# Order of batch 0's second value products in a fused sliding-attention and SiLU kernel

## The chip, the cores and the metric

The kernel runs on one core of one Trainium2 chip. The metric is the device time of one execution in microseconds, taken as the median of the timed runs. Engine names are those of the profile: PE is the matmul engine and PEld its weight load, DVE, ACT and POOL are the vector, scalar and GpSimd engines, SP issues the output stores.

## What is computed

There are 8 batches of 8 heads, 576 positions and 64 dimensions. Four heads use a plain window of 32 keys, four a strided window (every fourth key, 32 of them). The attention output, with its heads side by side, is the input of a two-layer block with SiLU between.

```python
scores = scale * np.matmul(q, k.transpose(0, 1, 3, 2))
mask_plain = (rel >= 0) & (rel < window)                                     # window = 32
mask_dil = (rel >= 0) & (rel < window * dilation) & (rel % dilation == 0)    # dilation = 4
masks = np.stack([mask_plain if h < H // 2 else mask_dil for h in range(H)], axis=0)
scores = np.where(masks[None, :, :, :], scores, -1000000000.0)
attn = np.exp(scores - np.max(scores, axis=-1, keepdims=True))
attn = attn / (np.sum(attn, axis=-1, keepdims=True) + 1e-09)
attn_out = np.matmul(attn, v)
x = np.ascontiguousarray(attn_out.transpose(0, 2, 1, 3)).reshape(B * S, H * D)
h = x @ w_in                       # 4608 x 512 by 512 x 2048
g = h * (1.0 / (1.0 + np.exp(-h)))
out = g @ w_out                    # 2048 x 512
```

## The kernel before, in words

The kernel goes through the batches in order. For each batch the main loop runs the first layer (16 blocks of 128 hidden channels, with SiLU on ACT) and the second layer; the attention of the batches to come is woven into it. What is woven in, and where, is written by hand: `plan_of(b)` files calls under step numbers with `at(step, function, arguments)`, and the layer code calls `plan(step)` ahead of each block. Nothing reorders afterwards: each engine executes its instructions in the order in which the Python code issued them, and waits on semaphores that the framework adds where one instruction needs another's result or its buffer.

Batch 0 comes first, so its attention is cut in two parts along the sequence: part 0 is the positions 0 to 255, part 1 the positions 256 to 575. `z = 0` are the plain heads, `z = 1` the strided ones. The steps of a part are scores, maximum, exponentials (ACT, L574 and L563), normalising (DVE, L596), turning the probabilities (DVE, L612, tile `pt`), the value products and the casts.

- `values0(z, part)` (def at L691) issues the products of `pt` with the values `vw` by `products` (matmul at L643): 64 small matmuls for (z 1, part 1), 44 for (z 0, part 1). The order inside is by key block and then by head. Heads 0 and 1 write the first of two PSUM tiles `x`, heads 2 and 3 the second.
- `finish0(z, part, copies)` (def at L706) copies the two `x` tiles to the f16 tile `xT[z]`, which layer 1 reads. L713 is the copy for z = 1, L718 that for z = 0. For (1, 1) the first tile is copied by ACT and the second by DVE; for (0, 1) both by DVE.
- `layer1_part(f, part, plan)` (def at L739) is layer 1 of batch 0 for one part: matmuls at L754, SiLU at L762. For part 0 one call covers four blocks of 128 channels and has 16 matmuls of 256 columns; it calls `plan` ahead of each block with the step `f + i - 16`. With f = 8 and i = 0 that is step -8, and i = 2 is step -6. For part 1 one call covers two blocks, 8 matmuls of 320 columns.

The calls of layer 1 stand in this order: part 0 with f = 0, 4 and 8; then part 1 with f = 0, 2, 4 and on to 14, with part 0's last call (f = 12) ahead of part 1's f = 12. Part 1's first matmuls thus need all four casts of part 1, and those of part 0 need none of them.

[...] Tiles of the pool `ps` (4 buffers of one bank) hold the `x` tiles, the transposes and the scores of later batches, and the `h` tiles of the very first layer 1 call; tiles of the pool `big` (2 buffers of two banks) hold all other `h` and `o` tiles. In the built program the tiles around the change lie as follows: `x` of (1, 1) in banks 7 and 4, `x` of (0, 1) in banks 6 and 4, the first call's `h` in banks 6 and 5. Bank 4 is used by the second tile of (1, 1) and by the second tile of (0, 1). So the third product of (0, 1), which is the first to write that tile, carries a wait for the DVE copy of the second tile of (1, 1), and its first product a wait for the SiLU that read the first `h`.

`loads_held` (L824) writes one element of `pt` of (1, 1) on POOL, which holds back the loads issued behind it until the products of (1, 1) have read that tile. The loads are the rest of batch 1's q and k, the last quarter of `w_in`, all of `w_out` and batch 1's v.

Of the kernel before, what the change touches and what calls it, by code (L numbers as in the profile page):

```python
# [29 lines left out]
def kernel(  # L30
# [778 lines left out]
    def transposes(at, b, z, step, copies=both):  # L809
        for which in (1, 0):  # L810
            if b >= DT[z]:
                at(step, turn_qk, b, z, which)
                continue
            at(step, transpose, b, z, which, copies)

    def later(at, b, z, steps, copies=(nc.vector.tensor_copy, nc.vector.tensor_copy)):

        for hi in (0, 1):
            at(steps[hi], normal, b, z, hi)
            at(steps[hi], turned, b, z, hi)  # L820
        at(steps[3], values, b, z)
        at(steps[3], finish, b, z, copies)
# [12 lines left out]
    def plan_of(b):  # L835
        ev = {}

        def at(s, fn, *args):
            ev.setdefault(s, []).append((fn, args))

        def all_exps(b, z):
            for hi in (0, 1):
                at(16, exps, b, z, hi)

        if b == 0:

            at(-8, values0, 1, 1)
            at(-8, loads_held)
            at(-8, finish0, 1, 1, (act, dve))
            at(-6, values0, 0, 1)  # L850
            at(-6, finish0, 0, 1)
            at(0, build_mask)
            at(1, load_qk, 2)
            transposes(at, 1, 1, 6)
            at(10, scores, 1, 1, 0)
            at(11, scores, 1, 1, 1)
            at(13, transpose, 1, 0, 1, both)
            at(15, transpose, 1, 0, 0, both)
            at(11, shift, 1, 1, 0)
            at(17, scores, 1, 0, 0)  # L860
            at(19, scores, 1, 0, 1)
            at(15, load_qk, 3)
            at(15, load_v, 2)
            all_exps(1, 1)
            for hi in (0, 1):
                at(20, exps, 1, 0, hi)
            later(at, 1, 1, (20, 21, 24, 27), (act, act))
            later(at, 1, 0, (23, 24, 28, 31), (act, dve))
        elif b == 1:
            at(16, load_v, 3)  # L870
            transposes(at, 2, 0, 4)
            transposes(at, 2, 1, 6)
            at(9, scores, 2, 0)
            transposes(at, 3, 0, 11, (dve, dve))
            at(17, load_qk, 4)
            at(15, scores, 2, 1)
            all_exps(2, 0)
            all_exps(2, 1)
            at(17, scores, 3, 0)
            later(at, 2, 0, (21, 24, 27, 28))  # L880
            at(22, shift, 3, 0, 0)
            at(22, exps, 3, 0, 0)
            at(22, exps, 3, 0, 1)
            later(at, 2, 1, (29, 30, 33, 34), both)
        else:
            if b + 2 < B:
                at(16, load_v, b + 2)
            if b + 1 < B:
                later(at, b + 1, 0, (0, 0, 4, 6))
                transposes(at, b + 1, 1, 7)  # L890
                if b + 3 < B:
                    at(16, load_qk, b + 3)
            if b + 2 < B:
                transposes(at, b + 2, 0, 14)
                at(19, scores, b + 2, 0)
                at(20, exps, b + 2, 0, 0)
                at(20, exps, b + 2, 0, 1)
            if b + 1 < B:
                at(12, scores, b + 1, 1)
                if b + 2 == B:  # L900
                    at(14, shift, b + 1, 1, 0)
                all_exps(b + 1, 1)
                later(at, b + 1, 1, (22, 23, 27, 28))

        def plan(s):
            for fn, args in ev.pop(s, ()):
                fn(*args)

        return plan
# [48 lines left out]
    for b in range(B):  # L958
        plan = plan_of(b)
        if b == 0:  # L960
            for f in range(0, 12, 4):
                layer1_part(f, 0, plan)
            for f in range(0, NFF, 2):
                if f == 12:
                    layer1_part(12, 0, plan)
                layer1_part(f, 1, plan)
        else:
            for f in range(NFF):
                plan(f)
                layer1(b, f)  # L970
        if b == 0:
            layer2_first(plan)
        else:
            layer2(b, plan)
        for s in range(NFF, 3 * NFF):
            plan(s)
# [30 lines left out]
```

## Time and profile before

| what | us |
|---|---|
| median of 3 runs | 304.52 (304.48 to 304.62) |
| the profiled execution | 305.81 |
| its span, first to last instruction | 303.8 |
| PE busy | 292.5 (96%) |
| ACT busy | 203.1 (67%) |
| DVE busy | 192.9 (63%) |
| POOL busy | 118.8 (39%) |

The span is the part of the profiled execution that the trace covers; 2.0 us of the 305.81 lie around it. The granted TensorE clock is 0.999 on average. The chain that ended last is 91% PE and 5% DMA. All the DMA waits in it come before 22.1 us: the loads of q and k and the first two quarters of `w_in`. From 22.1 us on it runs on PE.

In the timeline, a row is a run of equal instructions: its start, the time from the first one's start to the last one's end, engine, line, operation, tiles, shape and count. Brackets give the engine's idle time just before, and what ended it; "issue" stands for nothing that the profile shows.

### The profile page before, as it was taken

What the parts mean: (1) busy time and instruction counts of PE and PEld (TensorE: products, weight loads), DVE (VectorE), ACT (ScalarE), POOL (GpSimd) and SP (SyncE); (2) the same over time, 40 slices, a digit from 0 to 9 for tenths busy, and PEclk for the clock granted to TensorE, in tenths of its full rate; (3) what the DMA queues carried; (4) which work ended last, traced back from release to release, by engine and by line L of the source; (5) the groups of instructions that cost most, each with busy time, mean ns of one, the idle gap of its engine ahead of it and who ended that gap; (6) DMA issues with size and microseconds to landing.
All of it is one profiled execution on the core that took longest, in us unless ns stands there. A gap on an engine that the chain in (4) does not pass through costs nothing.

```text
span 303.8 us, 10280 instructions
## 1 busy us (share of the span) xinstructions
PE 292.5 (96%) x4395; PEld 185.9 (61%) x4395; DVE 192.9 (63%) x357; ACT 203.1 (67%) x683; POOL 118.8 (39%) x182
## 2 busy tenths in 40 slices
PE   2989999999999999999999999999999999999995
PEld 1656754677545774477644775478644775477543
DVE  1895469557997868866893768955893765800012
ACT  3677599775898659965894659976796558246200
POOL 8617326768997295336806086250000000000000
PEclk9999999999999999999999999999999999999999
DMA  8998999999999899399959199390002100210021
GB/s 100 142 196 135 193 205 124 220 154 145 132 163 198 93 71 130 113 111 40 124 72 184 38 60 131 112 121 2 2 37 106 37 2 12 95 37 0 9 97 69
DMA packets 113213, 30.47 MB, mean 100 GB/s; under 512 B 95520, under 2 KB 108688, under 8 KB 113168
## 3 DMA queue, kind: packets, MB, share of 16 engines
q0 software_dynamic: 107840, 20.38, 85.9%
q1 hardware_dynamic: 5328, 9.44, 8.7%
q8 instruction: 34, 0.56, 0.8%
q14 instruction: 11, 0.09, 0.1%
HBM read 40.75 MB, written 9.44 MB: 165 GB/s over the span
## 4 chain that ended last, share of the span: by engine, by line
PE 91%; DMA 5%; POOL 1%; issue 1%; DVE 0%; POOLq 0%
PE o L798 37%; PE h L727 37%; PE h L754 5%; PE o L774 5%; PE x L643 4%; DMA w_in<-in_moe_w_in_dram 3%; DMA gT<-in_q_dram 3%; PE s L364 2%; PE t L283 1%; POOL gT L135 1%; PE s L374 0%; PE ss L364 0%; PE s L390 0%; POOL w_in L191 0%; POOL vw L183 0%
## 5 line engine op out<-in xcount | busy, mean ns | idle before, releaser
L735 ACT ACTIVATE gT<-h 128x576 f16<-128x576 f32 x112 | 72.9, 651 | 63.6 <-PE h L727 63.4
L798 PE MATMUL o<-w_out,gT 128*128 128x512 f16 (+2 forms) x528 | 113.8, 373 | 0.0
L727 PE MATMUL h<-xT,w_in 128*128 128x288 f16 x896 | 113.2, 286 | 0.0
L727 PEld LDWEIGHTS <-w_in 128*128 128x128 f16 x896 | 86.6, 98 | 23.3
L798 PEld LDWEIGHTS <-gT 128*128 128x128 f16 x528 | 50.1, 98 | 56.0
L574 ACT ACTIVATE pe<-ms,nm 128x64 f32<-128x64 f32 x238 | 78.9, 333 | 0.1
L783 DVE COPY ob<-o 128x512 f32<-128x512 f32 (+2 forms) x35 | 23.0, 666 | 51.6 <-PE o L798 50.6
L574 ACT ACTIVATION_READ_ACCUMULATOR pe<-ms,nm 128x1 f32 x238 | 44.5, 187 | 0.0
L152 POOL DMA_DIRECT2D n<-in_k_dram x44 | 31.9, 732 | 26.5 <-DVE kC L337 25.1
L408 DVE SCALAR_TENSOR_TENSOR ms<-s,mask 128x512 f32<-128x512 f32 x28 | 19.2, 686 | 27.5 <-PE s L364 20.9
L152 POOL DMA_DIRECT2D n<-in_q_dram x44 | 31.9, 732 | 4.2 <-DMA n<-in_q_dram 3.5
L174 POOL DMA_DIRECT2D vw<-in_v_dram x32 | 18.3, 578 | 31.3 <-PE x L643 26.5
L596 DVE TENSOR_TENSOR pn<-pe,r 128x640 f16<-128x640 f32 (+2 forms) x32 | 25.3, 792 | 1.1
L183 POOL DMA_DIRECT2D vw<-in_v_dram x32 | 21.2, 667 | 11.5 <-DMA w_out<-in_moe_w_out_dram 8.4
L612 DVE STREAM_TRANSPOSE pt<-pn 128x640 f16<-128x640 f16 (+4 forms) x32 | 24.7, 772 | 1.1
L488 DVE TENSOR_REDUCE nm<-ms 128x10 f32<-128x640 f32 (+1 forms) x28 | 21.9, 786 | 0.9
L754 PE MATMUL h<-xT,w_in 128*128 128x256 f16 (+1 forms) x128 | 18.0, 291 | 1.2 <-DMA w_in<-in_moe_w_in_dram 0.9
L643 PEld LDWEIGHTS <-vw 32*64 32x64 f16 (+1 forms) x1264 | 12.8, 107 | 5.6 <-issue 5.2
L754 PEld LDWEIGHTS <-w_in 128*128 128x128 f16 x128 | 11.9, 99 | 6.0 <-DMA w_in<-in_moe_w_in_dram 2.1
L676 DVE CAST xT<-x 128x288 f16<-128x288 f32 x26 | 10.1, 450 | 8.2 <-PE x L643 8.2
L774 PE MATMUL o<-w_out,gT 128*128 128x512 f16 x64 | 14.7, 380 | 0.0
L643 PE MATMUL x<-pt,vw 32*64 32x64 f16 (+2 forms) x1264 | 14.6, 193 | 0.0
(94 smaller groups left out, 204.2 us busy)
## 6 DMA issues: line engine op xcount, KB each, us to landing
out_dram<-ob SPq DMA_DIRECT2D x35, 256.0 KB, 3.4
n<-in_k_dram POOLq DMA_DIRECT2D x24, 108.0 KB, 4.7
n<-in_q_dram POOLq DMA_DIRECT2D x24, 108.0 KB, 4.5
vw<-in_v_dram POOLq DMA_DIRECT2D x31, 80.0 KB, 3.9
vw<-in_v_dram POOLq DMA_DIRECT2D x32, 72.0 KB, 4.0
w_in<-in_moe_w_in_dram POOLq DMA_DIRECT2D x4, 512.0 KB, 8.3
w_out<-in_moe_w_out_dram POOLq DMA_DIRECT2D x4, 512.0 KB, 14.4
n<-in_k_dram POOLq DMA_DIRECT2D x20, 72.0 KB, 4.5
```

The lines of the kernel that those rows point to most:

```text
L152: nc.gpsimd.dma_start(out=qk[b, z, which][o : o + QB], in_=bass.AP((q, k)[which].tensor, (b * H + z * HH + half * HH // 2) * S * D + x * Q ...
L488: nc.vector.tensor_reduce(out=nm[:, 0:w], in_=ms[:, 0:w], axis=AX.X, op=ALU.max, negate=True)
L574: nc.scalar.activation(pe[:, t, :], src[t], AF.Exp, bias=a["nm", z, hi][:, t : t + 1], scale=k, accum_out=l[:, t : t + 1],)
L596: nc.vector.tensor_tensor(pn[:, 0:w], a["pe", z, hi][:, 0:w], r[:, 0:w, None].broadcast_to([P, w, KB]), ALU.mult)
L612: nc.vector.transpose(out, src)
L643: nc.tensor.matmul(x[h // 2][h % 2 * D : h % 2 * D + D, col : col + wd], vws[b % 2][r, NB + kb * DIL + c if z else kb], turned_cols(b, pt[ ...
L727: nc.tensor.matmul(h[:, half, 0:HS], w_in16[:, c, f * P : f * P + P], xT[c // 2][:, c % 2, half * HS : half * HS + HS], start=(c == cs[0]) ...
L735: nc.scalar.activation(gT[:, f, s0 : s0 + S].rearrange("p (a c) -> p a c", a=2), h[:, :, 0:HS], AF.Silu)
L754: nc.tensor.matmul(hs[i // m][:, i % m, 0 : c1 - c0], w_in16[:, c, (f + i) * P : (f + i + 1) * P], xT[c // 2][:, c % 2, c0:c1], start=(c = ...
L774: nc.tensor.matmul(o, gT[:, f, t * P : (t + 1) * P], w_out16[:, f, :], start=(f == 0), stop=(f == NFF - 1),)
L783: copy(ob, o)
L798: nc.tensor.matmul(o[:, 0, 0:m], gT[:, f, t * P : (t + 1) * P], w_out16[:, f, cols], start=(f == 0), stop=(f == NFF - 1),)
```

## The change

The products of (z 0, part 1) and their two casts are filed under step -8 instead of -6. They are thus issued directly behind the products of (1, 1), `loads_held` and the casts of (1, 1), ahead of all 16 matmuls of `layer1_part(8, 0)` instead of between the 8th and the 9th.

```diff
             at(-8, values0, 1, 1)
             at(-8, loads_held)
             at(-8, finish0, 1, 1, (act, dve))
-            at(-6, values0, 0, 1)
-            at(-6, finish0, 0, 1)
+            at(-8, values0, 0, 1)
+            at(-8, finish0, 0, 1)
             at(0, build_mask)
```

In the built program, DVE, ACT, POOL and SP have the same instructions in the same order as before. On PE the 44 pairs of weight load and matmul of (0, 1) stand ahead of the first 8 pairs of `layer1_part(8, 0)` instead of behind them. One separate wait instruction of PE (ahead of the first matmul of `layer1_part(8, 0)`) is gone. The PSUM banks are those of before.

## Prediction

> **What bounds the kernel now.** I read the page first: PE is busy 96% of the span, and the chain that ended last is PE for 91%.
>
> ```profile
> PE 292.5 (96%) x4395; PEld 185.9 (61%) x4395; DVE 192.9 (63%) x357; ACT 203.1 (67%) x683; POOL 118.8 (39%) x182
> PE 91%; DMA 5%; POOL 1%; issue 1%; DVE 0%; POOLq 0%
> ```
>
> So a change counts only if it moves PE's stream in time. Next I read the chain of waits in order of time over the stretch that is edited (start, us, what):
>
> ```profile
> 23.98 0.64 PE x L643 x61
> 24.62 1.05 PE h L754 x8
> 25.67 0.46 PE x L643 x44
> 26.12 0.87 PE h L754 x7
> 26.99 0.31 issue
> 27.30 1.37 PE h L754 x9
> ...
> 34.01 0.40 PE s L390 x39
> 34.41 0.17 issue
> 34.59 0.23 PE s L390 x9
> ```
>
> The strided products (61 of the 64 are in this row), 8 layer 1 matmuls, the 44 plain products, 7 more matmuls, a hole of 0.31 us, and then the 16th matmul, which is the first of the nine in the 27.30 row. The reader is to see that PE works without a break from 23.98 to 26.99 and that only 0.31 us are lost, and 0.17 us once more at 34.41. Last I read the timeline, for what the other engines do there:
>
> ```profile
> 23.66 2.00 ACT L762 ACTIVATE gT<-h 128x512 f16<-128x512 f32 x3
> 23.70 0.51 DVE L612 STREAM_TRANSPOSE pt<-pn 128x320 uint32<-128x320 uint32 x1
> 24.73 0.49 DVE L713 CAST xT<-x 128x320 f16<-128x320 f32 x1 [0.52 <-PE x L643]
> 25.54 0.44 ACT L713 CAST xT<-x 128x320 f16<-128x320 f32 x1
> 25.60 0.53 PE L643 MATMUL x<-pt,vw 32*64 32x32 f16 x44
> 26.05 0.94 PE L754 MATMUL h<-xT,w_in 128*128 128x256 f16 x7
> 26.18 0.89 DVE L718 CAST xT<-x 128x320 f16<-128x320 f32 x2 [0.97 <-PE x L643]
> 27.30 0.28 PE L754 MATMUL h<-xT,w_in 128*128 128x256 f16 x1 [0.31 <-issue]
> 27.62 1.02 ACT L762 ACTIVATE gT<-h 128x1024 f16<-128x1024 f32 x1 [1.64 <-PE h L754]
> 28.69 0.30 PE L754 MATMUL h<-xT,w_in 128*128 128x320 f16 x1
> ```
>
> The probabilities that the moved products read are turned by 24.21 (23.70 + 0.51), before the strided products end. The cast L713 on DVE runs from 24.73 to 25.22. It empties bank 4, into which the third moved product writes. Before, the 8 matmuls of layer 1 stood between the two, and the product (25.60) came 0.38 us after the bank was free. The two casts L718 end at 27.07.
>
> **The change part by part.** *Nothing is added or removed* except one wait instruction of PE, which I cost at nothing: it stood at 24.6, with the matmul behind it starting as soon as the products had drained. The 44 products keep their 0.45 us (25.60 to 26.05, start to the next matmul's start). The 8 matmuls keep their pace: 24.62 to 25.60 is 0.98 us for eight, of which some 0.11 us is the change to small tiles, so 0.11 us each. No DMA is moved. POOL's write of one element, behind which its loads queue, still waits for the strided products, whose place is unchanged; the 7.71 us that POOL waits before 24.18 stay, and so do its queue and SP's.
>
> *The wait that is now exposed.* Products one and two of the 44 go to bank 6, free since the first SiLU of 23.66 (24.26). The third waits for the DVE cast, so PE stands from about 24.5 to 25.22 and a release. Behind the waiting product stand the other 41 products and all 16 matmuls, none of which PE can put in its place; DVE's next instruction is the cast of these very products, and ACT's next SiLU needs the 16th matmul. DVE and ACT have nothing else to do there (the 0.97 and 1.64 us of idle time in their rows). The release itself is not shown for this pair. Its bounds: the shortest near row is the SiLU of 27.62 + 1.02 = 28.64, whose bank is written by a matmul at 28.69, 0.05 us later; the longest is a PE weight load at 9.48 behind an ACT copy that ended at 9.24, 0.24 us later. I take 0.05, since that row is also a matmul that waits for a PSUM bank while its weights are loaded. So the products go on at 25.27.
>
> *The sum.* 25.27 + 0.45 for the products and the change of tile size = 25.72, first matmul of layer 1. The 16th starts 15 x 0.11 = 1.65 us later, at 27.37. Before it started at 27.30. Shift: +0.07 us, and +0.26 with the long release. The same by differences: the products come 0.33 us earlier (25.60 to 25.27); eight more matmuls stand behind them, 0.87 us without their change of tile size; and the 16th no longer waits from 26.82 (26.05 + 7 x 0.11) to 27.30, 0.48 us. That is -0.33 + 0.87 - 0.48 = +0.06.
>
> *What the hole was.* The 16th matmul carries no wait, so the hole is not the casts: they end at 27.07, and the first instruction that needs them comes after it. PE's instruction stream explains it. The page counts 34 packets on the instruction queue of PE for 4395 + 4395 instructions, one for about 256:
>
> ```profile
> q8 instruction: 34, 0.56, 0.8%
> 27.29:34.58 7.29, 7.09 (x128) 4.85 (x128) 2.96 (x6) 5.45 (x8) 4.39 (x7) 1.00 1.07 159
> ```
>
> The second row is the stretch between the two holes: 128 matmuls and 128 loads, 256 instructions exactly. The two holes thus stand where PE goes from one block of 256 to the next. The packets themselves, by the trace's record of that queue, landed at 25.86 and 33.19, 1.44 and 1.40 us ahead of the two starts. The first was under way from 24.86, behind a border that PE passed at 23.27, in the part that is not edited; the 16th matmul's place in the stream changes by one instruction. So PE may not start it before 27.30 after the change either, and 27.37 is later than that: the hold costs nothing there, and no time can be won there.
>
> [...]
>
> *What comes behind.* The SiLU of these 16 matmuls and the matmul of 28.69 that waits for its bank move by the same 0.07 us; the four casts are done by 26.8 (25.7 + 0.1, two casts in 0.89), before anything needs them, so they are no bound. Of the 0.17 us at 34.41 I can't tell whether it is fixed in time (then it swallows the shift, and the span stays at 303.8) or follows PE's passing of the block before (then the shift goes through). I take the latter, as the packet's transfer (32.30) begins only behind that passing: 303.8 + 0.07 = 303.87. The profiled execution has 2.01 us around its span (305.81 against 303.8) and is 1.29 us above the median of the runs, which the change does not touch; against the median it is 304.52 + 0.07, or 304.6.
>
> **The rivals.** 0.2% is 0.61 us, about what a measurement of this kernel can tell from no change; so the line runs at 303.91 and 305.13.
>
> *Hidden anyway.* The hold at 34.59 is fixed in time: 34.41 + 0.07 is below 34.59, nothing is moved, 304.5. For it: 0.17 us is more than 0.07, and with the long release (0.26) only 0.09 is left. [...]
>
> *The wait isn't there (faster).* If the third product did not have to wait for the cast, products would run on from 24.45, end with the tile change at 24.45 + 0.45 = 24.90, and the 16th matmul would start at 26.55, 0.75 us earlier, if the block of instructions were there: 303.8. For it: the diff takes four changes of tile size down to two and the casts away from the first part 1 matmul. Against: bank 4 is written by both, and the built program has the wait; and the hold at 27.30 would keep the 16th matmul.
>
> *The instructions come later (slower).* PE's blocks are fetched one ahead among POOL's loads. POOL issues four loads of `w_out` from 27.69 on, just behind the hole at 27.30; they land some 2.55 us apart (POOL's waits for them end at 39.59, 42.13 and 44.72). If the shift puts a block's request behind one more of these, PE waits at 34.59 for 2.55 us more: 304.5 + 2.55 = 307.1, and part of one, half say, 305.8. It decides when the request slips by about 0.4 us (27.30 to 27.69). For it: three borders already cost time or nearly so. Against: 0.07 us, 0.26 at most.
>
> **How the numbers follow.** Forecast (wait for the cast, nearly paid back, carried through) 0.55, 304.6, own range 304.5 to 304.8. Hidden anyway 0.23, 304.5. Faster 0.09, 303.8. Slower 0.13, 305.8. The first two are both within 0.2%: 0.78. The range reaches to the faster case's line, 303.9, and a little past the slower line, 305.2, which leaves about 0.2 outside and holds both ends of the release.
>
> **What would show it.** In the timeline after: 2 or so products, then an idle gap of some 0.7 us ended by DVE's cast L713 at 25.22; the other products from about 25.27; 15 or 16 matmuls of L754 in one run from about 25.72; the 16th at 27.37; no hole of 0.31 us; DVE's two casts L718 between 25.8 and 26.8. If the strided products run into the plain ones without a gap, the wait is not there. If the hole at 27.30 is still there and at a later time, the fetch is the bound. If the stream is on time up to 34.4 and late afterwards, look at the hold of 34.59 and at the next one at 68.3.

## The result, and the profile after

The changed kernel takes 305.21 us (median of 13 runs, 304.72 to 306.85), the kernel before 304.48 us (13 runs, 303.81 to 304.87). The ratio is 1.0034, with a 95% interval of 1.0021 to 1.0047: slower, by 0.7 us. The forecast was 304.6 us with a range of 303.9 to 305.2, and no change as the likeliest outcome. The time lies only 0.01 us above that range, but the range reached so far up for the sake of the slower rival; the forecast itself is 0.6 us off.

The single profiled execution of the changed kernel took 305.16 us, with a span of 303.3 us. That span is 0.5 us *shorter* than the 303.8 us of the profile before. A comparison of these two pages alone thus has the wrong sign.

The chain of waits of the changed kernel, in order of time, over the edited stretch (start, us, what):

```profile
22.01 1.92 PE h L754 x16
23.93 0.72 PE x L643 x62
24.65 0.02 issue
24.67 0.50 DVE xT L713
25.17 0.04 issue
25.21 0.52 PE x L643 x41
25.73 2.94 PE h L754 x24
28.67 0.03 issue
28.70 2.33 PE h L754 x16
```

The chain leaves PE once: from 24.65 to 25.21 it runs over DVE's cast L713. This piece is new. Behind it, the products and 24 matmuls of layer 1 run without a hole. The timeline of the same stretch shows who waits:

```profile
24.67 0.49 DVE L713 CAST xT<-x 128x320 f16<-128x320 f32 x1 [0.73 <-PE x L643]
25.21 0.52 PE L643 MATMUL x<-pt,vw 32*64 32x32 f16 x42 [0.63 <-DVE xT L713]
25.67 4.55 PE L754 MATMUL h<-xT,w_in 128*128 128x256 f16 x34
25.78 0.89 DVE L718 CAST xT<-x 128x320 f16<-128x320 f32 x2 [0.62 <-PE x L643]
```

PE sits idle for 0.63 us ahead of the 42 products that are left of the 44. The release by the cast took 0.04 to 0.05 us (25.16 or 25.17 to 25.21), and the two casts L718 end at 26.67.

So the local figures that the prediction gave for this stretch came true, and the result still lay outside its range. The experiments were made to find out why.

### The profile page after: what moved, and what is told of

It reads as the page before. It is cut to its first block, busy times and chain, and to the rows that moved or that the text cites. A ratio compares the mean times of both kernels' runs of the same rounds, so it can differ in the third digit from the quotient of the medians.

```text
span 303.3 us, 10279 instructions
## 1 busy us (share of the span) xinstructions
PE 291.8 (96%) x4395; PEld 186.1 (61%) x4395; DVE 192.6 (63%) x357; ACT 202.9 (67%) x683; POOL 118.7 (39%) x182
## 4 chain that ended last, share of the span: by engine, by line
PE 91%; DMA 5%; POOL 1%; issue 1%; DVE 0%; POOLq 0%
PE o L798 37%; PE h L727 37%; PE h L754 5%; PE o L774 5%; PE x L643 4%; DMA w_in<-in_moe_w_in_dram 3%; DMA gT<-in_q_dram 2%; PE s L364 2%; PE t L283 1%; POOL gT L135 1%; PE s L374 0%; PE ss L364 0%; POOL w_in L191 0%; PE s L390 0%; POOL vw L183 0%
## 5 line engine op out<-in xcount | busy, mean ns | idle before, releaser
L727 PE MATMUL h<-xT,w_in 128*128 128x288 f16 x896 | 113.2, 286 | 0.0
L727 PEld LDWEIGHTS <-w_in 128*128 128x128 f16 x896 | 86.6, 98 | 23.3
L754 PE MATMUL h<-xT,w_in 128*128 128x256 f16 (+1 forms) x128 | 17.6, 291 | 1.3 <-DMA w_in<-in_moe_w_in_dram 1.3
L754 PEld LDWEIGHTS <-w_in 128*128 128x128 f16 x128 | 12.1, 99 | 5.6 <-DMA w_in<-in_moe_w_in_dram 2.3
```

What stands on the lines that cost most here:

```text
L727: nc.tensor.matmul(h[:, half, 0:HS], w_in16[:, c, f * P : f * P + P], xT[c // 2][:, c % 2, half * HS : half * HS + HS], start=(c == cs[0]) ...
L754: nc.tensor.matmul(hs[i // m][:, i % m, 0 : c1 - c0], w_in16[:, c, (f + i) * P : (f + i + 1) * P], xT[c // 2][:, c % 2, c0:c1], start=(c = ...
```

## The experiments

All traces can be put on one scale by counting from the 17th matmul of layer 1, the first one that needs the second quarter of `w_in`. It starts at 22.06 in the first trace of before and at 22.01 in that of the changed kernel. Two later points are used below: the 48th matmul (the last of `layer1_part(8, 0)`, the "16th" of the prediction) and the 57th (the first that waits for that call's SiLU).

### The two kernels again

Copies of both kernels, unchanged, were run for more traces and times.

before_again: 

> The kernel before once more, unchanged, for another profile. Theory A (the hold is not always there): the 0.31 us hole at 27.30 was a matter of that one execution; here the 16th matmul of L754 starts at 26.8 to 27.1 when counted with the first product at 23.91, the part 1 matmuls start by about 27.1, and the change then costs -0.33 + 0.87 = +0.54 us. Theory B (the hold stays, time is lost behind): the hole of about 0.3 us ends near 27.3 again, and the loss of the change lies behind 34 us. Ratio to before 1.000.

after_again: 

> The changed kernel once more, unchanged. Both theories: 0.63 us of idle PE ahead of the third plain product, ended by DVE's cast; 16th matmul 3.40 us behind the first strided product (27.31 against 23.91). Theory A: nothing else differs from before, so the trace behind 28 us has the same steps as in before, later by some 0.5 us. Theory B: a hold behind 34 us that before does not have. Ratio about 1.0025.

Measured: before_again 304.79 us against 304.43 for before, timed beside it (1.0013, 1.0003 to 1.0023); after_again 305.14 (1.0031, 1.0013 to 1.0049). A copy of the same program can thus come out 0.13% apart, which limits what such a ratio can tell.

The chain of waits of before_again, in order of time:

```profile
21.48 1.92 PE h L754 x16
23.40 0.63 PE x L643 x61
24.04 0.98 PE h L754 x8
25.02 0.46 PE x L643 x44
25.47 4.42 PE h L754 x32
```

This is to be held against the rows of before in the prediction. There, the 44 products were followed by 7 matmuls, 0.31 us of "issue", and the rest from 27.30. Here, the same 44 products are followed by 32 matmuls in one piece. The hole is not there. The 48th matmul starts 4.70 us behind the 17th, not 5.24. In after_again it starts 5.31 us behind, as in the first trace of the changed kernel. The 0.63 us of idle PE that were expected there are split: `w_in` came early (17th matmul at 21.07), the first two plain products waited 0.27 us for SiLU on ACT, and the third then 0.18 us for the cast. (The two products fill the time between.) In after_look3 it is 0.30 and 0.15 us.

Each of the two kernels was profiled three more times, to see which of the two executions of before is the rule.

before_look2: 

> The kernel before, one look. Theory A: the 16th matmul of step -8's call comes 4.70 us behind the 17th matmul of layer 1 (the first one behind the second quarter of w_in), without an idle gap, as in before_again, and not 5.24 us as in the profile of before.

before_look3: 

> The kernel before, another look. As before_look2: 4.70 us without the hold, 5.24 with it. With three looks without it the 27.30 of the first profile is the exception.

before_look4: 

> The kernel before, one more look: 4.70 to 4.85 us from the 17th to the 48th matmul without the hold, idle PE near 40 us between 0 and 0.9 us.

after_look2: 

> The changed kernel, one look. Counted from the 17th layer 1 matmul (the first behind the second quarter of w_in) the 33rd comes 3.66 us later, the 48th 5.31 us, against 2.5 to 2.6 and 4.7 to 4.8 in executions of before without the hold. If part of this is paid back at the third border (PE's idle time near 40 us, 0.01 to 0.88 us in before), that idle time is under 0.1 us here, as in after and after_again.

after_look3: 

> The changed kernel, another look: 3.66 and 5.31 us again, idle PE near 40 us under 0.1 us.

after_look4: 

> The changed kernel, a third look: 3.66 and 5.31 us again, idle PE near 40 us under 0.1 us. If it is 0.2 us or more here, the third border does not pay back the loss, and all of it goes through to the end.

Measured, with two later traces (before_third and after_third, below), in us:

| trace | 17th matmul at | 48th, from 17th | 57th, from 17th | idle PE near 40 us | idle PE near 68 us | span |
|---|---|---|---|---|---|---|
| before | 22.06 | 5.24 | 6.63 | 0.01 | 0.34 | 303.8 |
| before_again | 21.48 | 4.70 | 6.08 | 0.12 | 0.07 | 302.2 |
| before_look2 | 21.61 | 4.84 | 6.22 | 0.67 | 0.44 | 303.4 |
| before_look3 | 21.40 | 4.69 | 6.07 | under 0.04 | 0.17 | 301.9 |
| before_look4 | 21.66 | 4.71 | 6.09 | under 0.04 | 0.73 | 302.8 |
| before_third | 21.43 | 4.69 | 6.07 | under 0.04 | 0.09 | 301.8 |
| after | 22.01 | 5.31 | 6.69 | under 0.04 | 0.38 | 303.3 |
| after_again | 21.07 | 5.31 | 6.69 | under 0.04 | 0.50 | 302.5 |
| after_look2 | 21.82 | 5.31 | 6.69 | under 0.04 | 0.40 | 303.1 |
| after_look3 | 20.92 | 5.31 | 6.69 | under 0.04 | 0.67 | 302.7 |
| after_look4 | 22.48 | 5.30 | 6.69 | under 0.04 | 0.48 | 303.9 |
| after_third | 21.60 | 5.31 | 6.69 | under 0.04 | 0.41 | 303.1 |

Two things follow. The hole at 27.30, on which the prediction's sum stood, is in one of six executions of before. And the changed kernel takes 6.69 us from the 17th to the 57th matmul in all six of its traces, where before without the hole takes 6.07 to 6.22: the change costs 0.47 to 0.62 us at this place, every time.

Theory A (the hold is not always there) holds. Theory B asked for the hole at 27.30 in every execution of before and a new hold behind 34 us. The first part is refuted; the second is taken up under what stays open.

### The wait taken away: own_banks

The order of the change is kept. The plain products write the two PSUM tiles of the first layer 1 call (banks 6 and 5) in place of banks 6 and 4. The first added line stands in `layer1_part`, the others in `values0`.

```diff
+            att(0)["h00"] = hs
-            a["x"] = [ps.tile([P, 512], F32, tag="ps", name=f"x_0_{z}_{part}_{hp}") for hp in (0, 1)]
+            a["x"] = [t.rearrange("p a c -> p (a c)") for t in a["h00"]] if part and not z else [
+                ps.tile([P, 512], F32, tag="ps", name=f"x_0_{z}_{part}_{hp}") for hp in (0, 1)
+            ]
```

> The changed order, but the plain products write the two PSUM tiles of the first layer 1 call (banks 6 and 5) instead of banks 6 and 4, so that they wait for SiLU only and not for the DVE cast. If the wait for the cast is what the change costs, the 0.63 us of idle PE go to at most 0.1, and the time falls by 0.5 to 0.6 us against the changed kernel, to 304.6 or less; where the block of instructions is there in time it is below before by 0.2 to 0.4 us (304.1). If the cost lies behind 34 us or in the order itself (casts, ACT), it stays at 305.2.

Measured: 304.52 us (1.0000, 0.9988 to 1.0011), 0.62 below after_again, timed beside it. It is not below before, which the expectation had as a possibility. Its trace doesn't show the gain. `w_in` came early in it (17th matmul at 20.81), and PE waited for SiLU instead:

```profile
23.61 0.20 PE L643 MATMUL h<-pt,vw 32*64 32x32 f16 x2 [0.24 <-ACT gT L765]
24.10 0.52 PE L643 MATMUL h<-pt,vw 32*64 32x32 f16 x42 [0.29 <-ACT gT L765]
```

That is 0.53 us of idle PE where at most 0.1 was expected, and the 48th matmul comes 5.38 us behind the 17th, no sooner than in the changed kernel. So it was run again, side by side with the two kernels.

own_third: 

> Changed order with banks of their own, again. If the cast's wait is the cost: as before_third within 0.1%, 0.4 to 0.7 us below after_third. Trace: if w_in comes as in most executions (17th matmul at 21.4 or later), idle PE ahead of the plain products is under 0.15 us, and the 48th comes 4.7 to 4.9 us behind the 17th instead of 5.31; if w_in comes early (20.8), PE waits for SiLU, as in own_banks.

own_look: 

> The same kernel, one look: as own_third. 4.7 to 4.9 us from the 17th to the 48th matmul where the 17th starts at 21.4 or later, up to 5.4 where it starts at 20.8.

before_third: 

> The kernel before as a kernel of its own, in one call with the two others. 1.000 to 1.0015 against before; the trace has the 48th layer 1 matmul 4.70 to 4.85 us behind the 17th, or 5.24 with the hold.

after_third: 

> The changed kernel again. If the loss is real and not a matter of placing: 1.002 to 1.0035 against before, and 0.3 to 0.7 us above before_third. If it is placing, as with before_again: within 0.1% of before_third. Trace: 5.31 us from the 17th to the 48th matmul.

Measured, against 304.30 for before, timed beside them: before_third 304.42 us (1.0009, 0.9991 to 1.0027), own_third 304.52 (1.0010, 0.9999 to 1.0021), after_third 305.24 (1.0041, 1.0027 to 1.0054). after_third lies 0.82 us above before_third, a little more than the 0.3 to 0.7 expected; own_third lies 0.72 below after_third. The timeline of own_third:

```profile
23.76 0.70 PE L643 MATMUL x<-pt,vw 32*64 32x32 f16 x64
24.30 0.76 PE L643 MATMUL h<-pt,vw 32*64 32x32 f16 x44
24.57 0.49 DVE L715 CAST xT<-x 128x320 f16<-128x320 f32 x1 [0.63 <-PE x L643]
24.98 2.46 PE L757 MATMUL h<-xT,w_in 128*128 128x256 f16 x20
```

(The edit shifts the lines: the cast L713 is L715 here, and the matmul of layer 1 L757.) The plain products now start at 24.30, ahead of the cast's end at 25.06, and need no more than 0.05 us of idle PE on the way. The 17th matmul started at 21.91, so this is an execution with late `w_in`: the 48th comes 4.72 us behind it and the 57th 6.11, as in before. In own_look ACT ended its exponentials 0.38 us later (22.47 against 22.09); PE waited 0.29 us for SiLU, and the 48th came at 5.06, above the 4.9 expected.

One edit that leaves the order as the change made it, and only takes the plain products out of the bank that the cast holds, brings the time back in the timed runs, twice. So the loss hangs on the wait for the cast and not on the order alone. The three traces show how far this goes in one execution: against the changed kernel's 5.31 us to the 48th matmul, the whole delay is gone in own_third (4.72), 0.25 us of it in own_look (5.06), and none in own_banks (5.38), since in the last two the wait for SiLU takes the place of that for the cast.

### The wait made longer: act_bank

The second tile of the plain products was put into the bank that ACT empties behind three SiLUs, not into the one that DVE empties. The lines around the one shown are those of own_banks.

```diff
...
+            a["x"] = [a["h00"][0].rearrange("p a c -> p (a c)"), a["x"][0]] if part and not z else [
...
```

> The changed order, but the second tile of the plain products lies in the bank (7) that ACT empties behind three SiLUs, not in the one that DVE empties (4): the wait is made longer, as ACT's cast ended 0.55 us behind DVE's in the changed kernel (25.72 against 25.16). If the wait for the cast is what the change costs, idle PE ahead of the third product grows from 0.63 to about 1.2 us and the time by some 0.5 us, to 305.6 to 305.8. If other places set the time, it stays at 305.2.

Measured: 306.22 us (1.0056, 1.0038 to 1.0074; 6 runs). Its timeline on PE:

```profile
24.05 0.20 PE L643 MATMUL h<-pt,vw 32*64 32x32 f16 x2 [0.44 <-ACT gT L765]
25.77 0.20 PE L643 MATMUL x<-pt,vw 32*64 32x32 f16 x2 [1.52 <-ACT xT L715]
26.29 5.01 PE L757 MATMUL h<-xT,w_in 128*128 128x256 f16 x26
```

Idle PE is 1.52 us, more than the 1.2 expected. ACT's cast ended at 25.72, as in the changed kernel, but `w_in` came early in this trace (17th matmul at 21.05), so the products stood ready sooner. The time is 0.4 to 0.6 above what was expected too. The windows tell why (us, then each engine's busy time and count, then the granted clock, DMA share and GB/s):

```profile
24.00:26.00 2.00, 0.43 (x31) 0.38 (x35) 0.32 (x1) 1.72 (x3) 2.00 (x4) 1.00 0.69 96
26.00:28.00 2.00, 2.00 (x46) 1.46 (x34) 1.48 (x5) 0.00 (x0) 2.00 (x3) 0.52 0.93 138
28.00:30.00 2.00, 2.00 (x13) 1.44 (x12) 0.81 (x3) 0.21 (x1) 2.00 (x4) 0.63 1.18 173
```

The third number from the right is the granted clock. In the trace it falls to half from 26.07 to 29.48, 3.41 us, behind the long idle time. The six runs fall into two groups: three with a mean clock of 0.994, the traced one among them, took 306.55 to 306.75 us, three with 1.0 took 305.64 to 305.89. The second group is the wait alone, within the 305.6 to 305.8 expected but for one run at 305.89. So the time follows the length of the wait: 304.5 without it, 305.2 with the DVE cast, 305.7 with the ACT cast at full clock (three runs), and 1 us more where the clock falls.

### Half way: step_minus7 and own_banks_minus7

```diff
-            at(-6, values0, 0, 1)
-            at(-6, finish0, 0, 1)
+            at(-7, values0, 0, 1)
+            at(-7, finish0, 0, 1)
```

step_minus7: 

> The plain products one block of layer 1 later than in the change (step -7: behind 4 matmuls instead of 0 or 8). The 4 matmuls take 0.44 us, so the wait for the cast shrinks from 0.63 to some 0.1 us. Theory A: 304.5 to 304.7, near before. Theory B (time lost behind 34 us through a shift of the stream): anything between the two kernels.

own_banks_minus7 is the same step with the banks of own_banks: 

> Plain products behind 4 matmuls of layer 1 (step -7) and in banks of their own (6 and 5): neither the cast nor SiLU (over by then) holds them, and their casts end some 0.4 us earlier than in before. No idle PE from the strided products to part 1. Theory A: local time as in an execution of before without the hold (16th matmul 4.70 us behind the 33rd, 4.8 at most), total 304.3 to 304.6, not clearly below before.

Measured: step_minus7 304.78 us (1.0004, 0.9989 to 1.0019; 304.5 to 304.7 was expected), own_banks_minus7 304.58 (1.0007, 0.9989 to 1.0024). In step_minus7's timeline, the cast ends at 25.11 and the products follow without idle time:

```profile
24.62 0.49 DVE L713 CAST xT<-x 128x320 f16<-128x320 f32 x1 [0.69 <-PE x L643]
25.14 0.55 PE L643 MATMUL x<-pt,vw 32*64 32x32 f16 x44
```

own_banks_minus7's chain has no step over DVE or ACT:

```profile
24.56 0.64 PE x L643 x62
25.19 0.54 PE h L757 x4
25.74 0.46 PE h L643 x43
26.19 2.50 PE h L757 x20
```

Its 48th matmul comes 4.69 us behind the 17th, as in before without the hold. So four matmuls between the two groups of products cover the cast (step_minus7), and where the cast is not waited for at all, the earlier casts L718 bring nothing (own_banks_minus7). No version that beats before was found.

## Why the prediction was wrong, point by point

**The wait that is exposed, and its size: right.** The third product waits for the cast, PE's products go on at 25.21 (25.27 predicted), the first matmul of layer 1 comes at 25.67 (25.72), the 48th at 27.32 (27.37). The release of 0.05 us was well chosen. The casts L718 ran from 25.78 to 26.67 (25.8 to 26.8 predicted). Removing the wait and lengthening it moved the time as this mechanism asks: 305.2 us with it, 304.5 without it, 305.7 where it was longer and the clock full.

**What the shift is counted against: the step that failed.** The prediction set 27.37 against 27.30, the start of that matmul in the one profiled execution of before, and said that "PE may not start it before 27.30 after the change either". Its own differences had the true answer: -0.33 + 0.87 - 0.48 = +0.06, where the -0.48 is the hole that the change was to cover. Against that one execution the shift is as forecast, 5.31 - 5.24 = +0.07. But the hole was taken for a property of the kernel. In five of six traces of before there is no such hole, and the sum is -0.33 + 0.87 = +0.54, against 0.47 to 0.62 in the traces. The prediction had noted that this execution was 1.29 us above the median of the runs, and left that aside as something "which the change does not touch". The hole was part of what made it long.

**What the hole was: compatible, not tested.** The hole of 0.31 us stands, with the one at 34.59, at the two ends of a stretch of 256 instructions (128 matmuls and 128 loads, in the first trace of before). In the first trace PE's packet landed at 25.86 and the matmul started 1.44 us later; in before_again it landed at 24.27, 1.91 us ahead of the 48th matmul at 26.18, and there is no hole. In the five traces of before without the hole the packet landed 1.51 to 1.94 us ahead. That agrees with the reading of the prediction, but no run moved the border or the packet, so what caused the hole is the author's reading and was not shown.

**The second hole, at 34.59: also a matter of that execution.** None of the other eleven traces of the two kernels has one there of 0.04 us or more. So it could neither swallow the shift nor pass it on.

**The slower rival: wrong mechanism.** It needed a block of instructions to slip behind a load of `w_out` and gave 305.8. The time (305.21) came out half way between the forecast and this rival, but the loss stands at the cast, and in the changed kernel PE has no idle time at 34 us. The faster rival named the right condition, the wait for bank 4: with that wait taken away the loss is gone. Its 303.8 was counted against the 27.30 too, and own_banks came out at 304.5.

**What stays open.** From the 17th matmul to the end, the six traces of before take 281.04 us on average and those of the changed kernel 281.45: 0.41, not the full 0.6. The starts of the matmuls tell where the difference arises. Up to the 57th the changed kernel loses 0.50 us on average. From there to the 128th, the last of L754, it wins 0.24 back (12.28 against 12.05 us): before sometimes stands still near 40 us, for up to 0.67 us, and once at 34.59, the changed kernel never for 0.04. From there to the 80th matmul of L727 it loses another 0.15 (28.57 against 28.71), with the idle time near 68 us, 0.31 on average in before and 0.47 in the changed kernel. Behind that, all twelve take 233.98 to 234.02 us, so no part of the loss lies there. Both places vary by several tenths from one execution to the next, so six traces a side give the 0.24 and the 0.15 only roughly, and no run shows what they come from. The three traces with banks of their own have 0.47 to 0.54 us of idle time near 68 us too, so that part does not seem to hang on the wait for the cast. A new hold behind 34 us, as theory B has it, was not found; only the longer idle time near 68 us could stand for it.

The second quarter of `w_in` explains next to none of it: the 17th matmul starts at 21.61 on average in before and at 21.65 in the changed kernel. The medians of the timed runs differ by 0.71 to 0.94 us from those of before, and by 0.35 and 0.82 from those of its copies before_again and before_third, so the size of the loss is known to a few tenths only.

## What to carry to other kernels

Before a change is priced against a hole in the profile, see whether the hole belongs to the kernel or to that execution: a profiled execution well above the median of the runs (here 1.29 us) says that some of its waits may not be usual, and work that is moved to fill such a wait costs time in all executions without it (here 0.47 to 0.62 us against five of the six traces of before). And when two groups of small products are set next to each other, look at which PSUM bank the second group writes: the matmuls between the groups (here eight, 0.98 us) were the cover of the copy that empties it (0.49 us).

## What the runs showed of the hardware

In the traced run of act_bank the clock fell to half for 3.41 us, behind PE idle times of 0.44 and 1.52 us (1.96 in all) within 2.2 us; two more of its six runs have the same mean clock, 0.994, and are as long. In the changed kernel, with 0.63 us, the mean clock of every run stayed at 0.998 or above. What made the clock fall, and why three of the six runs of act_bank kept a mean clock of 1.0, no run shows.
